# Constant matmuls at the start, early first products, and an earlier third batch in a fused attention and feed-forward kernel

## The chip, the cores and the metric

One core of a Trainium2 chip. The metric is device time in microseconds (us) of one execution. The kernel before took 272.6 us (median of three, 272.22 to 273.03). PE is TensorE, PEld its weight loads, DVE is VectorE, ACT is ScalarE, POOL is GpSimd. "Cold" and "warm" stand for the TensorE clock at half and at full speed (0.5 and 1.0 in the traces' clock record; in the kernel before, weight loads for 512-column matmuls start 0.427 us apart before the record's rise at 27.13 us and 0.214 after it).

## The reference, cut to what matters

Eight batches of attention, eight heads, 576 positions, head size 64. Four heads ("plain") see a window of 32 keys; four ("dilated") see 32 keys at every fourth place. The result, 4608 rows of 512, goes through `((x @ w1) * (x @ w2)) @ w3 @ w_out`.

```python
mask_plain = (rel >= 0) & (rel < window)
mask_dil = (rel >= 0) & (rel < window * dilation) & (rel % dilation == 0)
...
a = x @ w1
b = x @ w2
h = a * b @ w3
return (h @ w_out)
```

## The kernel before

The kernel multiplies w3 by w_out once (`wf`). A token block of 512 rows then needs 64 matmuls of 512 columns for a and b (`ffn1`, f = 0 to 7, four channel groups c each) and 32 for the output (`ffn2`). Each batch's attention is four steps (d0, d1 dilated, p0, p1 plain): scores, exponential, values, normalization on DVE, then six transposes on PE and a copy into `XT`. In profile lines `qt` and `kt` are a step's transposed queries and keys, `vd` and `vp` its values, `xo` its normalized output. Channels 2 and 3 of `XT` are the dilated heads, 0 and 1 the plain ones. The first batch runs ahead of everything. Later steps are laid among the feed-forward matmuls by numbered points, two per f or output block.

```python
def first_batch():
    ...                      # scores of d0, d1, p0; values of d0; scores of p1 ...
    d0.to_channels()
    p0.values_of_pair(0)
    p0.values_of_pair(1)
    d1.to_channels()
    p1.values_of_pair(0)
    p1.values_of_pair(1)
    p0.to_channels()         # all four through one PSUM tile, ps_x, and ACT
    p1.to_channels()
...
def ffn1(t, f, point, lo=0, hi=TB):
    for w_sb in (w1_sb, w2_sb):
        point()
        ps = bank()[:, 0 : hi - lo]
        for c in range(DCH):
            nc.tensor.matmul(out=ps, lhsT=w_sb[:, c, f * P : (f + 1) * P], rhs=XT[:, c, ...],
                             start=(c == 0), stop=(c == DCH - 1))
...
(26, d0.values),             # second batch: (point, what)
(28, transpose_qk, 1, 0, 0),
(28, d0.to_channels),
(28, d1.values),
(29, transpose_qk, 1, 0, 1),
(30, p0.scores),
```

The softmax here doesn't subtract the row's maximum and nothing guards it: scores larger than these inputs give would overflow.

## Time and profile before

The time splits at three places: the first weight load of the first feed-forward block, the first load of w3 (the fused weights begin) and the first load of `gt` (the first output block begins).

| stretch before | from | to | length, us |
|---|---|---|---|
| first batch | 0 | 22.49 | 22.49 |
| first feed-forward block | 22.49 | 38.88 | 16.39 |
| fused weights, second batch | 38.88 | 62.17 | 23.3 |
| rest | 62.17 | 270.16 | 207.99 |

The stretch view of the kernel before gives, for each stretch, its length, the busy time of PE, PEld, DVE, ACT and POOL in this order (number of instructions in brackets), the granted clock, the time that DMA packets took as a share of the 16 DMA engines' time (over 1 where packets overlap) and the rate in GB/s:

```profile
0.00:22.49 22.49, 14.47 (x183) 9.32 (x184) 13.48 (x56) 8.40 (x12) 16.99 (x31) 1.00 1.26 161
22.49:38.88 16.39, 15.66 (x68) 6.75 (x66) 4.84 (x7) 5.19 (x9) 4.63 (x7) 1.00 1.17 209
38.88:62.17 23.29, 20.79 (x261) 11.94 (x260) 16.21 (x32) 9.28 (x11) 12.71 (x17) 1.00 1.52 194
62.17:270.20 208.03, 201.35 (x1846) 99.58 (x1844) 123.85 (x234) 90.81 (x137) 23.49 (x30) 1.00 0.55 91
```

The first number after each length is PE. It is idle 8.0 us in the first row, 2.5 in the third and 6.7 in the last. The clock column's 1.00 in the first two rows is no reading, as the prediction works out: the record begins at 27.13 us.

### The profile page before, as it was taken

The numbers are of one execution on the slowest core, as the hardware profiler recorded it, in microseconds if no ns is written. First come the engines' busy times: TensorE is split into PE (matmuls) and PEld (weight loads), VectorE is DVE, ScalarE is ACT, GpSimd is POOL, SyncE is SP. The second block draws the span as 40 slices with busy tenths as digits, with TensorE's granted clock in tenths as the row PEclk, the third lists the DMA queues.
The fourth block names the chain that finished last, engine by engine and source line by source line (L and its number), as shares of the span: only waits on it lengthen the run. The fifth ranks groups of instructions, "written<-read, shape, count | busy, mean of one in ns | idle before, by whom it ended". The sixth has DMA issues, their size and how long they took to land.

```text
span 270.2 us, 5648 instructions
## 1 busy us (share of the span) xinstructions
PE 252.3 (93%) x2352; PEld 127.6 (47%) x2352; DVE 158.4 (59%) x329; ACT 113.7 (42%) x167; POOL 57.8 (21%) x84
## 2 busy tenths in 40 slices
PE   0897999979988899999999999999999999999993
PEld 0473445545444455455555455554545544444441
DVE  5552446777598777775776678577836642422420
ACT  1443332533455345544553553454454424323331
POOL 8962236534026113310611060000000000000000
PEclk9999999999999999999999999999999999999999
DMA  6999999999959986969597886310040022014013
GB/s 113 163 193 206 210 206 201 195 181 199 222 87 142 91 177 138 103 126 181 72 76 130 194 72 45 109 50 0 4 130 27 0 62 96 0 39 120 0 38 117
DMA packets 51817, 30.50 MB, mean 113 GB/s; under 512 B 37968, under 2 KB 42064, under 8 KB 51792
## 3 DMA queue, kind: packets, MB, share of 16 engines
q0 software_dynamic: 46160, 20.70, 61.9%
q1 hardware_dynamic: 5632, 9.44, 10.9%
q8 instruction: 18, 0.29, 0.5%
q14 instruction: 7, 0.06, 0.1%
HBM read 41.39 MB, written 9.44 MB: 188 GB/s over the span
## 4 chain that ended last, share of the span: by engine, by line
PE 87%; DVE 7%; ACT 2%; DMA 2%; issue 1%; POOL 0%; POOLq 0%; DVEq 0%
PE f L502 45%; PE f L535 23%; PE ps_a L264 4%; PE ps_x L355 4%; PE f L565 3%; PE ps_a L306 3%; DMA kn<-in_k_dram 2%; PE ps_s L264 2%; DVE xo L314 2%; PE ps_s L280 1%; ACT XT L370 1%; ACT et L294 1%; DVE qt L236 1%; DVE kt L229 1%; DVE et L295 1%; DVE gt L513 1%
## 5 line engine op out<-in xcount | busy, mean ns | idle before, releaser
L502 PE MATMUL f<-XT,w_sb 128*128 128x512 bf16 x576 | 135.9, 383 | 0.7 <-ACT XT L370 0.7
L502 PEld LDWEIGHTS <-w_sb 128*128 128x128 bf16 x576 | 53.4, 98 | 60.1 <-issue 3.5
L513 DVE TENSOR_TENSOR gt<-f,asb 128x512 bf16<-128x512 f32 x72 | 49.4, 687 | 48.3 <-PE f L502 44.0
L512 ACT CAST asb<-f 128x512 bf16<-128x512 f32 x72 | 42.1, 585 | 67.2 <-PE f L502 67.2
L535 PE MATMUL f<-wf_sb,gt 128*128 128x512 bf16 x288 | 68.0, 379 | 0.0
L543 ACT COPY osb<-f 128x512 f32<-128x512 f32 x36 | 21.0, 585 | 50.8 <-PE f L535 50.8
L535 PEld LDWEIGHTS <-gt 128*128 128x128 bf16 x288 | 26.4, 98 | 28.5 <-DVE gt L513 0.4
L294 ACT ACTIVATE et<-ps_a 128x1152 bf16<-128x1152 f32 x28 | 31.7, 1134 | 14.0 <-PE ps_a L264 14.0
L138 POOL DMA_DIRECT2D vd<-in_v_dram x32 | 21.3, 672 | 41.9 <-PE ps_a L306 32.4
L314 DVE TENSOR_TENSOR xo<-ps_a,rcp 96x768 bf16<-96x768 f32 x28 | 26.7, 953 | 1.0
L264 PEld LDWEIGHTS <-kt 32*128 32x128 bf16 x768 | 12.2, 97 | 22.5 <-issue 16.9
L236 DVE STREAM_TRANSPOSE qt<-qn 128x160 uint32<-128x160 uint32 (+1 forms) x64 | 19.6, 423 | 1.3 <-DMA qn<-in_q_dram 1.3
L306 PEld LDWEIGHTS <-et 128*128 128x128 bf16 x384 | 16.9, 102 | 6.9 <-issue 0.5
L295 DVE TENSOR_TENSOR et<-et,mask_pl 128x1152 bf16<-128x1152 bf16 x14 | 10.6, 758 | 12.8 <-ACT et L294 12.8
L295 DVE TENSOR_TENSOR et<-et,mask_di 128x1152 bf16<-128x1152 bf16 x14 | 10.6, 756 | 10.4 <-ACT et L294 10.4
L565 PE MATMUL f<-wo_sb,w3T 128*128 128x512 bf16 x64 | 16.0, 380 | 0.7 <-ACT w3T L557 0.7
L264 PE MATMUL ps_a<-qt,kt 32*128 32x96 bf16 x672 | 12.4, 202 | 4.1 <-DVE xo L314 2.3
L355 PEld LDWEIGHTS <-xo 96*128 96x128 bf16 x192 | 12.3, 102 | 7.7 <-issue 1.1
L313 DVE RECIPROCAL rcp<-ps_a 96x12 f32<-96x12 f32 x28 | 6.3, 224 | 15.4 <-PE ps_a L306 15.4
L355 PE MATMUL ps_x<-ident,xo 96*128 96x96 bf16 x192 | 14.4, 214 | 0.9 <-ACT XT L370 0.7
L114 POOL DMA_DIRECT2D qn<-in_q_dram x10 | 6.6, 662 | 30.5 <-DVE qt L236 26.1
L370 ACT COPY XT<-ps_x 128x576 bf16<-128x576 bf16 x18 | 11.6, 642 | 2.7 <-PE ps_x L355 2.4
(51 smaller groups left out, 129.2 us busy)
## 6 DMA issues: line engine op xcount, KB each, us to landing
qn<-in_q_dram POOLq DMA_DIRECT2D x6, 576.0 KB, 5.5
kn<-in_k_dram POOLq DMA_DIRECT2D x6, 576.0 KB, 8.3
w3n<-in_moe_w_dram POOLq DMA_DIRECT2D x4, 512.0 KB, 17.0
out_dram<-osb SPq DMA_DIRECT2D x8, 256.0 KB, 2.4
vp<-in_v_dram POOLq DMA_DIRECT2D x5, 384.0 KB, 6.3
out_dram<-osb SPq DMA_DIRECT2D x8, 224.0 KB, 2.3
out_dram<-osb SPq DMA_DIRECT2D x8, 192.0 KB, 2.9
out_dram<-osb SPq DMA_DIRECT2D x8, 160.0 KB, 2.6
```

Source lines behind the costliest of these rows:

```text
L236: nc.vector.transpose(out=bass.AP(tensor=o.tensor, offset=o.offset + at, ap=[o.ap[0], [1, n], [9, 16], [step, 2]],), in_=t[:, a0 : a0 + 4 ...
L264: nc.tensor.matmul(out=bank_of(h)[:, c0 : c0 + 96], lhsT=kt[prt, 96 * m : 96 * m + P, c], rhs=rhs, start=(start and c == 0), stop=(c == 1 ...
L294: nc.scalar.activation(out=ev, in_=ps_a[:, :, 0:HALF], func=ACT.Exp, scale=scale)
L295: nc.vector.tensor_tensor(out=ev, in0=ev, in1=mk.unsqueeze(1).to_broadcast([P, 4, HALF]), op=AL.mult)
L306: nc.tensor.matmul(out=out, lhsT=self.et[:, c0 : c0 + P], rhs=rhs, start=True, stop=True)
L314: nc.vector.tensor_tensor(out=xo[0:96].rearrange("p (n k) d -> p n k d", n=n), in0=ov[0:96, :, :, x0 : x0 + D], in1=rcp[0:96].unsqueeze(3) ...
L355: nc.tensor.transpose(out=xo, in_=self.xo[0:96, hp, 2 * m : 2 * m + 2, :], identity=ident[0:96, 0:96],)
L502: nc.tensor.matmul(out=ps, lhsT=w_sb[:, c, f * P : (f + 1) * P], rhs=XT[:, c, t0 + lo : t0 + hi], start=(c == 0), stop=(c == DCH - 1),)
L512: nc.scalar.copy(out=a_sb[:, 0 : hi - lo], in_=ps)
L513: nc.vector.tensor_tensor(out=gts[t][:, f, lo:hi], in0=pss[1], in1=a_sb[:, 0 : hi - lo], op=AL.mult)
L535: nc.tensor.matmul(out=y, lhsT=gts[t][:, f, tb * P : (tb + 1) * P], rhs=wf_sb[:, f, :], start=(f == 0), stop=(f == KFF - 1),)
L565: nc.tensor.matmul(out=wf_ps[ft], lhsT=w3T[ft][:, g, :], rhs=wo_sb[:, g, :], start=(g == 0), stop=(g == KFF - 1),)
```

## The change

It has four parts: 16 constant matmuls that raise the clock early; the first two f of block 0 begun with the dilated channels alone, with p1's transposes in a bank of their own and copied by DVE; w3's first part loaded ahead of wo; and the schedule of the second and third batch moved up. Smaller moves that go with them (the values' PSUM banks, the first fused transposes into `ps_x`, the channel order 2, 3, 0, 1 everywhere) stand in the kernel alone.

```diff
+    def warm_up(n):
+        ps = bank()
+        for _ in range(n):
+            nc.tensor.matmul(out=ps, lhsT=warm[:, 0:P], rhs=warm, start=True, stop=True)
...
     def const_vector():
+        nc.vector.memset(warm, 1.0)
...
-        p0.to_channels()
-        p1.to_channels()
+        pool = four_banks()
+        for f in range(2):
+            for i in range(2):
+                begin(f, i, pool.tile([P, TB], F32, name=f"ps_b{f}{i}"))
+            if f == 0:
+                p0.to_channels()
+        p1.to_channels(bank().bitcast(BF16), nc.vector.tensor_copy)
...
-            (28, transpose_qk, 1, 0, 0),
+            (26, transpose_qk, 1, 0, 0),
+            (27, transpose_qk, 1, 0, 1),
...
-            (29, transpose_qk, 1, 0, 1),
...
+            (36, transpose_qk, 2, 1, 0),
             (38, p1.to_channels),
+            (38, transpose_qk, 2, 1, 1),
...
-            if i == lo:
-                later(transpose_qk, b, 1, 0)
-                later(transpose_qk, b, 1, 1)
...
+    def begin(f, i, ps):
+        begun[f, i] = ps
+        ffn1_half(0, f, (w1_sb, w2_sb)[i], (2, 3), begun[f, i])
...
+    warm_up(16)
...
+    load_w3(0)
     load_wo(0)
     load_wo(1)
-    load_w3(0)
...
-    marks = [(40, n0)]
+    marks = [(39, n0)]
```

## The prediction

> **What bounds the kernel now.** I read the page first, then the timeline of each engine over the first 100 us, then when each load landed. The page says that TensorE (PE) is the bound: busy 93% of a 270.2 us span, and the chain that ended last is 87% PE. From 100 us on, PE is busy in all of every stretch, and the change leaves that work alone. What can be won lies in the first 100 us.
>
> ```profile
> PE   0897999979988899999999999999999999999993
> PEld 0473445545444455455555455554545544444441
> DVE  5552446777598777775776678577836642422420
> ACT  1443332533455345544553553454454424323331
> ...
> DMA  6999999999959986969597886310040022014013
> ```
>
> These are tenths busy in 40 slices of 6.8 us. PE's gaps are all in the first 14 slices. The DMA engines are full from 5 us to about 65 us, at some 200 GB/s. "Busy" hides a second loss, which the weight loads of the first feed-forward block give away:
>
> ```profile
> 23.88 0.15 PEld L502 LDWEIGHTS <-w_sb 128*128 128x128 bf16 x1 [0.27 <-issue]
> 24.31 0.15 PEld L502 LDWEIGHTS <-w_sb 128*128 128x128 bf16 x1 [0.27 <-issue]
> ...
> 26.44 0.15 PEld L502 LDWEIGHTS <-w_sb 128*128 128x128 bf16 x1 [0.28 <-issue]
> 26.87 0.15 PEld L502 LDWEIGHTS <-w_sb 128*128 128x128 bf16 x1 [0.27 <-issue]
> 27.22 11.54 PEld L502 LDWEIGHTS <-w_sb 128*128 128x128 bf16 x54 [0.20 <-issue]
> ```
>
> The columns are start, length, engine, line, operation. Each load goes with one 512-column matmul. Up to 27.1 us they start 0.427 us apart; the next 54 take 11.54 us, 0.214 each. So PE runs at half speed until 27 us, although the page's clock row shows full speed throughout (the trace's clock record begins only at 27.13 us). The small attention matmuls between 7.8 and 18.2 us, back to back, did not raise it. The cost in the first block is its 15.75 us for 64 matmuls against 64 x 0.216 = 13.8, so 1.9 us; in the attention before it about half of each matmul.
>
> The third loss is the end of the first batch, a ping-pong of PE and ScalarE on one PSUM tile:
>
> ```profile
> 20.77 0.64 PE L355 MATMUL ps_x<-ident,xo 96*128 96x96 bf16 x6
> 21.44 0.64 ACT L370 COPY XT<-ps_x 128x576 bf16<-128x576 bf16 x1 [0.73 <-PE ps_x L355]
> 22.13 0.64 PE L355 MATMUL ps_x<-ident,xo 96*128 96x96 bf16 x6 [0.73 <-ACT XT L370]
> 22.81 0.64 ACT L370 COPY XT<-ps_x 128x576 bf16<-128x576 bf16 x1 [0.73 <-PE ps_x L355]
> 23.50 2.72 PE L502 MATMUL f<-XT,w_sb 128*128 128x512 bf16 x6 [0.73 <-ACT XT L370]
> ```
>
> Later PE stands still for kt of the second batch, and for VectorE's normalization of the third:
>
> ```profile
> 58.67 0.44 PE L264 MATMUL ps_a<-qt,kt 32*128 32x96 bf16 x24 [1.84 <-DVE kt L229]
> ...
> 79.36 0.44 PE L264 MATMUL ps_a<-qt,kt 32*128 32x96 bf16 x24 [0.76 <-DVE xo L314]
> ...
> 84.73 0.45 PE L264 MATMUL ps_a<-qt,kt 32*128 32x96 bf16 x24 [0.75 <-DVE xo L314]
> ...
> 90.11 0.45 PE L264 MATMUL ps_a<-qt,kt 32*128 32x96 bf16 x24 [0.75 <-DVE xo L314]
> ```
>
> [...] dense matmuls from 23.50, change at 27.13, 3.6 us later. [...] measured 427 and 214 to 216. [...] No trace here shows what load of small matmuls keeps a raised clock up; that is my main doubt.
>
> **The change, part by part.**
>
> *Warm-up.* VectorE fills a 128x512 tile first (near the 0.27 us of the trace's 32x256-word fill), so PE can start 16 matmuls at about 1.15 us instead of waiting for the first mask at 4.41. By the spacing above, all cold is 16 x 0.427 = 6.8 us; with the rise after some 5 us, 12 x 0.427 + 4 x 0.216 = 6.0. They end at 7.2 (at worst 8.0), and kt is ready only at 7.75. So they are hidden, and the scores then run warm.
>
> *First batch, if the clock stays up.* Scores need 0.6 to 0.65 us per pair instead of 1.18, then ScalarE's exponentials (0.65 each) set the pace. The plain heads' scores wait for kt, whose transpose runs 10.71 to 11.97 behind the load of k, so they gain only 12.54 - 12.0 = 0.5 us. The values of the plain heads need v, which landed at 15.88 us in the trace; before, PE came to them at 18.47. So they go at 15.9: 2.5 us won, the rest forbidden by DMA. The second dilated copy to XT then ends near 17.3 (before: 20.7).
>
> *Begun products.* After the split, 8 of the 64 matmuls (channels 2 and 3, the dilated heads) of f = 0 and 1 go into the four banks freed by the scores, among the plain heads' transposes; the last copy has its own bank and VectorE. The first weight slices landed at 17.22 (w1) and 18.56 (w2), so the second half-product waits to 18.56. Then: its 2 matmuls to 19.0, p0's six transposes to 19.3 (copy beside it to 19.95), 4 matmuls to 20.15, p1's transposes to 20.45, copy to 21.1. The other 56 matmuls take 56 x 0.216 = 12.1 us: end at 33.2 to 33.3, against 39.25. Later weights (w1 23.78, w2 26.33 for f = 4) come in time: f = 4 begins at 21.1 + 24 x 0.216 = 26.3. **Won: 5.9 us.**
>
> *Fused weights and second batch.* w3's first part now goes ahead of wo; the three parts trade landings 28.87, 31.40 and 33.91, in time for 33.3. The next w3 parts landed at 36.37, 41.69 and 46.20; PE would need them at about 36.6, 41.6 and 46.8, so there is no slack but no real wait. k of the second batch landed at 49.02; its transpose stands earlier in VectorE's order and ends near 50.5 instead of 58.6, where PE needs it at 50.9. So the 1.84 us wait goes, but VectorE sits on these loads with casts queued behind, which costs PE some 0.5 us. **Won: 1.3 us**, the stretch shrinking from 23.15 to about 21.9.
>
> *Third batch sooner.* Scores of the third batch move into the end of the first output block, and the matmuls between values and next scores go from 4 to 8 twice; 4 x 0.216 = 0.86 us covers two of the 0.75 us waits. The first wait (0.76) stays or grows: two transposes (2.2 us) lie in VectorE's queue ahead of the normalization in both kernels. **Won: about 1.1 us.**
>
> *Sum*: 5.9 + 1.3 + 1.1 = 8.3 us. The rest of the run has the same instructions. 272.6 - 8.3 = 264.3.
>
> **The rivals.**
> 1. *The clock falls back before the dense matmuls.* For: 10 us of small matmuls at full issue left it low, and in the new kernel PE idles from 10.4 to 12 and works half the time after. If it falls at once, the first batch runs as before up to d1's copy, with that at 20.2 to 20.7; the begun products cost 0.427 each, and the 56 end at about 37.8: 1.45 us won, and with nearly 2 us for the kt wait and 1.1 for the third batch about 4.7 in all, 267.9. If it falls only near 15 us, behind the wait for v, the loss is about 1.4 us: 265.7. [...]
> 2. *Loads take over.* The DMA engines are full to 65 us, so PE 6 us earlier meets landings that do not move. I counted v, w2 and k; if w3 or the third batch's q (54.3) and k (57.1) also bite, 1 to 2 us go: 266.
> 3. *VectorE becomes the bound* between 47 and 70 us: busy 8.1 of 10 us in 50 to 60 before, and the same work goes into less time. A wait of 1.5 us instead of 0.76 before the third batch's plain scores: 265.
>
> Nothing added lies on the path of the last 170 us, so slower is very unlikely.
>
> **Range and chances.** I give the warm case half, a late fall 30%, an early fall 20%: 0.5 x 264.3 + 0.3 x 265.7 + 0.2 x 267.9 = 265.4; the warm case being the most likely, I choose 264.9. The 2% mark is 267.1, near the early-fall case alone, so faster gets 0.84. The low end is the warm case with every wait gone (1.9 us more), the high end the early fall.
>
> **What would show it.** Warm-up matmuls from about 1.2 us whose spacing falls to 0.216; score matmuls at about half of 0.59 us per dozen; the plain values released by v at about 15.9; a PE wait on w_sb before the second begun product; the first fused-weight transpose near 33.3; no kt wait near 51; one wait on xo instead of three after 60. Spacing of 0.427 in the begun products means rival 1; waits on w3n or qn mean rival 2; a longer span after 100 us would break the whole account.

The spacings in ns are those of 512-column matmuls in the profile of the kernel before: 0.427 us up to 27.1 us, then 54 loads in 11.54 us, or 0.214 each; from 224.60 us on, 64 matmuls take 13.81 us, or 0.216 each, which the sums use. That the clock would rise after some 5 us of constant matmuls was my estimate; the trace shows one rise, 3.6 us after the dense matmuls began.

## The result, and the profile after

The changed kernel took 265.88 us (median of four: 265.95, 265.93, 265.83, 263.61) against 272.81 (272.22 to 273.16). The ratio is 0.9728, 95% interval 0.9673 to 0.9783. Ratios here are the mean time of one kernel's runs over that of the other's of the same rounds, so not quite the ratio of the medians. Executions over 1.5% slower than the fastest of the same kernel are left out of the means. Three runs lie within 0.12 us with a mean granted clock of 0.981. The fourth is 2.3 us faster with 1.000.

The stretch view of the changed kernel (a 0.981 run), same columns:

```profile
0.00:19.37 19.37, 16.40 (x188) 9.55 (x189) 12.18 (x52) 7.51 (x11) 15.23 (x28) 0.82 1.26 154
19.37:35.88 16.51, 15.62 (x79) 7.32 (x79) 7.03 (x15) 5.45 (x10) 5.18 (x8) 0.91 1.21 209
35.88:57.88 22.00, 20.57 (x257) 12.01 (x260) 16.11 (x32) 9.28 (x11) 10.71 (x14) 1.00 1.42 196
57.88:264.20 206.32, 198.76 (x1816) 99.61 (x1844) 123.77 (x234) 90.37 (x137) 26.64 (x34) 1.00 0.59 96
```

The first two stretches together end 3.00 us sooner (38.88 to 35.88), the third is 1.29 shorter (23.30 to 22.01) and the rest 1.69 (207.99 to 206.30). The sum is 5.98, all of 270.16 - 264.19 = 5.97 but for rounding. The clock column now shows a loss in the first two rows. The page's slices of 6.6 us show where:

```profile
PE   7798999999899999999999999999999999999993
...
PEclk9957999999999999999999999999999999999999
```

The clock is up, then down in the third and fourth slice, then up. The trace's clock record gives the moments: full speed from 5.43 us, half from 12.26, full again from 22.50. The timeline of PE weight loads (start, length) and then of PE matmuls shows the same in the spacing:

```profile
4.85 0.15 PEld L179 LDWEIGHTS <-warm 128*128 128x128 bf16 x1 [0.28 <-issue]
5.28 1.26 PEld L179 LDWEIGHTS <-warm 128*128 128x128 bf16 x6 [0.28 <-issue]
```

```profile
11.77 0.43 PE L275 MATMUL ps_s<-qt,kt 32*128 32x96 bf16 x12 [0.78 <-DVE kt L240]
...
12.64 0.66 PE L275 MATMUL ps_s<-qt,kt 32*128 32x96 bf16 x12
...
17.39 0.86 PE L317 MATMUL f<-vp,et 128*128 128x65 bf16 x12
...
20.48 1.06 PE L509 MATMUL ps_b<-XT,w_sb 128*128 128x512 bf16 x2 [0.22 <-issue]
...
23.99 1.90 PE L509 MATMUL ps_b<-XT,w_sb 128*128 128x512 bf16 x8 [0.55 <-DVE XT L380]
```

The last six warm-up loads take 1.26 us, 0.21 each, where those before stood 0.43 apart. A dozen score matmuls took 0.43 us at 11.77 and 0.66 at 12.64. The plain values at 17.39 waited for nothing: v had landed at 16.77, but PE, cold again, was still busy with the scores and the first transposes. Five of the eight begun matmuls ran cold too, and a sixth in part. The waits further on, from the same timeline:

```profile
54.38 0.45 PE L275 MATMUL ps_a<-qt,kt 32*128 32x96 bf16 x24 [0.56 <-DVE xo L325]
...
72.47 0.44 PE L275 MATMUL ps_a<-qt,kt 32*128 32x96 bf16 x24 [0.94 <-DVE xo L325]
...
77.90 0.44 PE L275 MATMUL ps_a<-qt,kt 32*128 32x96 bf16 x24
...
83.32 0.44 PE L275 MATMUL ps_a<-qt,kt 32*128 32x96 bf16 x24
```

The 1.84 us wait for kt has become 0.56 for the normalization (xo), which DVE takes up after kt. Of three waits on xo in the third batch, one is left, somewhat longer.

### The profile page after: what moved, and what is told of

It is laid out like the page before. It is cut to its first block, busy times and chain, and to the rows that moved or that the text cites. A ratio compares the mean times of both kernels' runs of the same rounds, so it can differ in the third digit from the quotient of the medians.

```text
span 264.2 us, 5646 instructions
## 1 busy us (share of the span) xinstructions
PE 251.4 (95%) x2332; PEld 128.5 (49%) x2368; DVE 159.1 (60%) x331; ACT 112.6 (43%) x166; POOL 57.8 (22%) x84
## 4 chain that ended last, share of the span: by engine, by line
PE 86%; DVE 5%; DMA 2%; ACT 2%; issue 2%; POOL 1%; POOLq 0%
PE f L509 45%; PE f L560 23%; PE ps_a L275 4%; PE ps_a L317 3%; PE f L591 3%; PE ps_x L366 3%; DMA kn<-in_k_dram 2%; PE ps_b L509 2%; DVE xo L325 1%; DVE kt L240 1%; DVE qt L247 1%; ACT et L305 1%; DVE et L306 1%; PE ps_s L275 1%; PE f L317 1%
## 5 line engine op out<-in xcount | busy, mean ns | idle before, releaser
L509 PE MATMUL f<-XT,w_sb 128*128 128x512 bf16 x538 | 128.9, 379 | 1.3 <-issue 0.2
L540 DVE TENSOR_TENSOR gt<-f,asb 128x512 bf16<-128x512 f32 x70 | 48.1, 687 | 39.5 <-PE f L509 35.2
L539 ACT CAST asb<-f 128x512 bf16<-128x512 f32 x70 | 41.0, 586 | 62.5 <-PE f L509 59.8
L560 PE MATMUL f<-wf_sb,gt 128*128 128x512 bf16 x279 | 66.3, 379 | 1.0 <-issue 0.8
L140 POOL DMA_DIRECT2D vd<-in_v_dram x32 | 21.3, 670 | 43.0 <-PE ps_a L317 33.3
L275 PEld LDWEIGHTS <-kt 32*128 32x128 bf16 x768 | 11.4, 94 | 17.6 <-issue 14.1
L591 PE MATMUL f<-wo_sb,w3T 128*128 128x512 bf16 x60 | 15.4, 380 | 0.9 <-ACT w3T L583 0.7
L366 PE MATMUL ps_x<-ident,xo 96*128 96x96 bf16 x186 | 13.8, 213 | 0.1
L380 ACT COPY XT<-ps_x 128x576 bf16<-128x576 bf16 x17 | 10.9, 643 | 3.5 <-PE ps_x L366 3.4
```

Of the source, the lines that this page charges most:

```text
L275: nc.tensor.matmul(out=bank_of(h)[:, c0 : c0 + 96], lhsT=kt[prt, 96 * m : 96 * m + P, c], rhs=rhs, start=(start and c == 0), stop=(c == 1 ...
L366: nc.tensor.transpose(out=xo, in_=self.xo[0:96, hp, 2 * m : 2 * m + 2, :], identity=ident[0:96, 0:96],)
L539: nc.scalar.copy(out=a_sb, in_=ps)
L540: nc.vector.tensor_tensor(out=gts[t][:, f], in0=pss[1], in1=a_sb, op=AL.mult)
L560: nc.tensor.matmul(out=y, lhsT=gts[t][:, f, tb * P : (tb + 1) * P], rhs=wf_sb[:, f, :], start=(f == 0), stop=(f == KFF - 1),)
L591: nc.tensor.matmul(out=wf_ps[ft], lhsT=w3T[ft][:, g, :], rhs=wo_sb[:, g, :], start=(g == 0), stop=(g == KFF - 1),)
```

## The experiments

They ran in three calls (e0 to e3, e4 to e7, e8 to e11). Each kernel ran six times, beside eleven runs of the kernel before in each call, whose means were 272.29, 272.04 and 271.82 us.

**Theory A.** The clock falls in the first batch in most executions (in the profile after at 12.26 us, 6.83 us after its rise), because PE is too thinly filled there. This costs the changed kernel some 2 us, and the schedule of batches two and three gives a fixed 3 us. **Rivals:** the loads set the pace, or the warm-up alone carries the gain.

**e0: the changed kernel again.**

> The changed kernel once more, beside the three runs of this call. Theory A (the TensorE clock falls in the first batch in most executions[...] and stays up in some): two levels, most near 265.9 us with a mean granted clock of 0.98, some near 263.6 us with 1.00, nothing between. Theory B (the 263.61 us was a chance of the loads): times scattered between 263.5 and 266.5 without tie to the clock.

Measured, with mean clock: 263.23 (1.000), 264.57 (0.986), 264.83 (0.986), 265.04 (0.987), 265.85 (0.981), 266.31 us (0.981); ratio 0.9732. There are three levels, not two, and they go with the clock. In the 0.986 profile the clock was up from 6.60 us, down from 13.43, up from 20.25: down for 6.83 us where the 0.981 profile had 10.24. The scatter follows the clock. Of ten runs of the changed kernel, two kept it. (e5 and e6 below leave the first batch as it is; two of six runs of each show 0.998 or more, which makes six of 22.)

**e1: no warm-up.**

```diff
-        nc.vector.memset(warm, 1.0)
...
-    warm_up(16)
```

> The changed kernel without its 16 constant matmuls and their fill. Theory A: where the clock has fallen at 12.3 us anyway, the warm-up saved only the 0.8 us by which the plain scores began sooner, and some of the raise of the clock for the begun products; so about 267 us (266.5 to 268), the clock rising near 24 us, all executions on one level. Theory B (the warm-up carries the gain): over 269 us.

Measured 266.31 us (266.03 to 267.23), ratio 0.9785. It is on one level, as theory A says, but the median is 0.2 us under the expected range and the rise came at 22.52 us, not near 24. The mean, 266.45, is 1.5 us above the changed kernel's 264.97. The clock record begins with that rise and shows no fall in the first batch.

**e2: the kernel before plus the warm-up alone.**

```diff
+        nc.vector.memset(warm, 1.0)
...
+    warm_up(16)          # into a bank of the values
```

> The kernel before plus only the fill and the 16 constant matmuls. Theory A: clock up near 5.5 us and down again near 12.3 us, the first block still begun cold, plain scores 0.8 us sooner: 271.5 to 272.2 us, the same within 2%. If the clock should hold, 3 us more: 268 to 269. Theory B (the warm-up carries the gain): under 268 us.

Measured 269.2 us (268.48 to 271.18), ratio 0.9893. This missed all that was expected but the "should hold" case, which is not quite what happened either: in the profile the clock was up from 4.29 to 17.94 us, past most of the first batch, and down from there to 24.77, over the start of the first block. It fell behind a wait of PE for v (to 16.47), the place that the prediction's late fall had. I had taken the fall at 12.3 us as given; its place shifts from run to run. With the clock up to 17.94, the block ended at 36.38 instead of 38.88. The means give 272.29 - 269.39 = 2.90 us for the warm-up alone, and only 1.5 us on top of the other parts. The two overlap: both bring the first block forward.

**e3: seventeen more constant matmuls inside the first batch.**

```diff
+    def hold(n):
+        for _ in range(n):
+            nc.tensor.matmul(out=ps_x.bitcast(F32), lhsT=warm[:, 0:P], rhs=warm, start=True, stop=True)
...
+        hold(1)   # behind each of the first three score groups
+        hold(4)   # behind the fourth
+        hold(2)   # behind p0's first, d0's values, d1's first values
+        hold(4)   # ahead of d0.to_channels
```

> The changed kernel plus 17 more constant matmuls spread over the first batch (one to four at a time, behind the score and value groups, into the transpose tile while that is unused)[...]. Theory A: the clock stays up from about 5.5 us in every execution; the fillers cost nothing on the path, which waits there for k and v; the first block ends near 34 us instead of 36.1, and the time is 263 to 263.8 us in all runs. Rival (loads set the pace, the clock is beside the point): clock up but still 265.5 us or more. Rival (fillers delay the scores): over 266 us.

Measured 265.03 us (264.85 to 265.81), clocks 0.997 to 1.000, ratio 0.9738. The clock held in all six and the spread shrank, but the time is no better. The fillers are in the way. In DVE's timeline kt of the plain heads was ready at 11.22; the four fillers at 11.20 hold PE to 12.07:

```profile
10.83 0.43 PE L281 MATMUL ps_s<-qt,kt 32*128 32x96 bf16 x12
11.20 1.04 PE L185 MATMUL ps_x<-warm 128*128 128x512 bf16 x4
12.07 0.41 PE L297 MATMUL ps_s<-neg_pl,ident 128*128 128x288 bf16 x2
```

No wait is left anywhere from 8 to 18 us in that timeline: PE itself is the path, fillers included. The block ended at 34.97. So the rival that fillers delay the scores was right in kind.

**e4: no begun products.**

```diff
-                begin(f, i, pool.tile([P, TB], F32, name=f"ps_b{f}{i}"))
+                pool.tile([P, TB], F32, name=f"ps_b{f}{i}")
```

> The changed kernel with no product begun early: all 64 matmuls of the first block after the plain heads' copies (the split over two transpose tiles and the copy on VectorE stay). Theory (the begun products fill the time of the copies and let the clock rise earlier): the block starts near 21 us instead of 19.5, pays some 1.9 us of half clock inside, and ends 0.8 to 1.5 us later than in the changed kernel; about 266.3 us. Rival (they only move work that waits for the weights anyway): no difference beyond 0.3 us from the changed kernel's 265 to 265.9.

Measured 265.39 us, but spread over 263.40 to 267.33 with clocks from 0.978 to 1.000; ratio 0.9756. Inconclusive: the clock's levels cover the difference sought. The profiled run, at 0.979, ended the block at 36.20, 0.32 later than the changed kernel's. e8 asks again with the clock held.

**e5: the third batch as late as before.**

```diff
-            (36, transpose_qk, 2, 1, 0),
-            (38, transpose_qk, 2, 1, 1),
+            if i == lo:
+                later(transpose_qk, b, 1, 0)
+                later(transpose_qk, b, 1, 1)
-    marks = [(39, n0)]
+    marks = [(40, n0)]
```

> The changed kernel with the third batch begun as late as before (its two dilated transposes and its mark put back). Theory: the stretch from the first output matmul to the end, 206.30 us in three profiles of the changed kernel, goes back to about 207.8 (207.99 and 208.02 before), the three waits of some 0.75 us on the normalization come back, and the first two stretches stay: near 266.8 us. Rival (an earlier first block alone removes those waits, as the loads are then no longer late): under 206.8.

Measured 266.51 us (265.65 to 268.04), ratio 0.9799. The rest is 207.99 us in its profile, to the hundredth what it was before, and PE's timeline has the three waits again:

```profile
74.02 0.44 PE L275 MATMUL ps_a<-qt,kt 32*128 32x96 bf16 x24 [0.75 <-DVE xo L325]
...
79.39 0.45 PE L275 MATMUL ps_a<-qt,kt 32*128 32x96 bf16 x24 [0.74 <-DVE xo L325]
...
84.77 0.44 PE L275 MATMUL ps_a<-qt,kt 32*128 32x96 bf16 x24 [0.75 <-DVE xo L325]
```

The earlier third batch is worth 1.69 us in that stretch, and no other part of the change gives it.

**e6: the second batch's plain transposes at their old points.**

```diff
-            (26, transpose_qk, 1, 0, 0),
-            (27, transpose_qk, 1, 0, 1),
+            (28, transpose_qk, 1, 0, 0),
...
+            (29, transpose_qk, 1, 0, 1),
```

> The changed kernel with the second batch's plain transposes back at their old places (points 28 and 29 instead of 26 and 27). Theory: the stretch of the fused weights, 22.01 us in every changed profile, goes back to 23.2 (23.30 before), with the wait on kt of 1.5 to 1.9 us again; near 266.4 us. Rival (the wait went because the first block ended earlier or because w3 came first): stays at 22.0.

Measured 264.73, 265.41, 267.20 and 268.26 us in four runs, mean 266.40, ratio 0.9793; two more, 268.93 and 269.31 with clocks 0.974 and 0.971. The stretch of the fused weights is 23.51 us, and PE's timeline shows the wait in full:

```profile
53.82 0.44 PE L275 MATMUL ps_a<-qt,kt 32*128 32x96 bf16 x24 [1.84 <-DVE kt L240]
```

So the place in DVE's order makes the 1.3 us (1.50 between these two profiles). The k rows were there in time in both: DVE began that transpose without a wait.

This profile is also the only one of the changed kernel's own first batch with the clock held (up from 4.76 us to the end). The block began at 17.67 and ended at 33.81, and PE met a load:

```profile
19.39 0.61 PE L509 MATMUL ps_b<-XT,w_sb 128*128 128x512 bf16 x2 [0.96 <-DMA w_sb<-in_moe_w_dram]
```

**e7: a longer start and seven fillers where PE waits.**

```diff
-    warm_up(16)
+    warm_up(19)
...
         d1.scores_of_pair(1)
+        hold(4)
...
         d1.values_of_pair(1)
+        hold(3)
```

> The changed kernel with 19 constant matmuls at the start instead of 16 and only 7 more inside, where PE waits anyway: 4 behind the dilated scores, 3 before the first transposes. Theory A: the 17 fillers of the last trial held the clock but cost over 1 us on the path, since the block ended at 34.97 with the clock up, where 33.5 is what the fastest execution of the changed kernel leaves. With few fillers the clock stays up in most executions, the block ends near 33.8 us: 263.2 to 264.2 us, steady. Rival (so few do not hold the clock): [...] two levels as in the changed kernel, median 265.

Measured 263.94 us (263.25 to 264.22), clocks 0.996 to 1.000, ratio 0.9701 (0.9660 to 0.9741). Time and clock are as theory A says. The gain over the changed kernel (264.94 in e0, of another call) is about 1 us, with overlapping intervals; that the spread is smaller is plain. Its first two stretches:

```profile
0.00:17.76 17.76, 14.93 (x195) 8.24 (x198) 11.69 (x51) 7.26 (x11) 15.11 (x28) 1.00 1.25 150
17.76:33.15 15.39, 14.37 (x81) 6.78 (x79) 7.34 (x15) 5.68 (x10) 4.58 (x8) 1.00 1.24 207
```

The block ends at 33.15, sooner than the 33.8 expected here, where the prediction's warm case had 33.2 to 33.3; the later stretches are 22.02 and 206.3 as in the changed kernel.

**e8: e7 without begun products** (the edit of e4 on e7).

> The held clock of e7 without any product begun early. Theory (with the clock up, eight begun matmuls of 0.216 us fill only what the copies leave, and they in turn push the plain transposes back): the first block starts near 19.6 us and ends within 0.5 us of e7's 33.15; time 263.8 to 264.5 us, not told apart from e7's 263.94. Rival (the begun products are a main part of the gain): 265 us or more.

Measured 264.07 us; the four runs with clocks of 0.998 or more took 263.31 to 264.27, two with 0.991 and 0.992 took 265.37 and 266.26; ratio 0.9729. With the clock up, the begun products are worth nothing that these runs resolve: the block started at 19.57 and ended at 33.51, 0.36 after e7's. That the clock sagged in two of six runs, and in none of e7's, may mean that they help to keep it; six runs don't settle it.

**e9: e7 with wo ahead of w3.**

```diff
-    load_w3(0)
     load_wo(0)
     load_wo(1)
+    load_w3(0)
```

> The held clock of e7 with wo loaded ahead of w3's first part, as before the change. Theory: in e7 the block ends at 33.15 and w3's first part landed at 28.53; behind wo it would land where wo's second half did, near 33.6, so the first fused transpose waits 0.3 to 1.4 us: 264.2 to 265.2 us, with a wait on w3n in the profile and the span of that stretch up from 22.01. Rival (the order is of no account): 263.94 within 0.2.

Measured 263.87 us (263.39 to 265.57), ratio 0.9714: as a median no different from e7. The profiled run was the longest of the six, at 265.57, and shows where it waited:

```profile
16.54 0.49 PE L323 MATMUL f<-vp,et 128*128 128x65 bf16 x11 [0.28 <-DMA vp<-in_v_dram]
...
19.21 0.61 PE L517 MATMUL ps_b<-XT,w_sb 128*128 128x512 bf16 x2 [0.52 <-DMA w_sb<-in_moe_w_dram]
...
35.66 0.62 PE L585 MATMUL ps_x<-ident,w3n 128*128 128x128 bf16 x8 [1.35 <-DMA w3n<-in_moe_w_dram]
```

Here v landed at 16.50, w2 at 19.17 and w3 at 35.62 us, and PE, warm, met all three. In the changed kernel's profile v (16.77) and w2 (19.45) were no sooner, but with the new order w3 landed at 29.69; so the order guards against the third wait. The other five runs, 263.39 to 263.89, show no cost. By its number the rival was right: 263.94 within 0.2. The wait that the theory expected is there in the one profile, but ahead of the fused stretch, which at 21.82 us did not grow.

**e10: e7 with one more begun half-product.**

```diff
         p1.to_channels(bank().bitcast(BF16), nc.vector.tensor_copy)
+        begin(2, 0, bank())
```

> e7 plus one more begun half-product (f = 2, w1), in a free bank behind the last transposes, where PE waits 0.55 us for VectorE's copy. Theory: two matmuls of 0.216 us go into that wait, as w1's second slice landed at 19.52: 0.4 us off e7, 263.3 to 263.7 us. Rival (the slice lands late in many executions, or the copy is delayed): no gain.

Measured 263.3 us (262.91 to 264.24), clocks 0.998 to 1.000, ratio 0.9695 (0.9654 to 0.9736). The block ends at 32.78, 0.37 sooner than e7's. It has the lowest median here, but its lead on e7, of another call, and on the changed kernel is within the intervals.

**e11: nineteen constant matmuls at the start, none inside.**

> The changed kernel with 19 constant matmuls at the start and none inside: parts e7. Theory A [...]: two levels remain, clocks from 0.98 to 1.00, median 264.5 to 265.5. Rival (the longer start alone holds the clock): all at 263.3 to 264.2 with clocks over 0.995.

Measured 264.41 us: 263.06, 263.33 and 263.85 with clocks of 0.996 or more, 264.97, 265.02 and 265.81 with 0.986, 0.994 and 0.981; ratio 0.9725. The longer start alone does not hold the clock. With fillers inside and begun products it held in all 24 runs of e3, e7, e9 and e10, and e3 did it with the short start; without the begun products (e8) in four of six. This profile, with the clock up to 259.64 us, again meets v, which landed at 15.85, and the second weight slice:

```profile
15.89 0.49 PE L317 MATMUL f<-vp,et 128*128 128x65 bf16 x11 [0.47 <-DMA vp<-in_v_dram]
...
18.60 0.61 PE L509 MATMUL ps_b<-XT,w_sb 128*128 128x512 bf16 x2 [0.63 <-DMA w_sb<-in_moe_w_dram]
```

## Why the prediction was right or wrong

The time, 265.88, lies between the warm case with every wait gone (262.4) and the early fall (267.9), and within 1 us of 264.9. "Faster by over 2%" was right for the median. That the middle number fits so well is in part luck: the clock fell more often than allowed for, and the held runs came out some 0.9 us below their 264.3, which offsets it. (The early-fall sum has a slip: 1.45 + 2 + 1.1 is 4.55, not 4.7.) Step by step:

- **Warm-up.** Right in kind. PE began at 1.46 us instead of 1.15, since the fill took 0.48 us and not 0.27. The rise came at 5.43, when PE had run nothing but these matmuls of ones since 1.46; the last warm-up matmul was done near 7.0, and kt was ready just after 7.8. It was hidden.
- **"First batch, if the clock stays up."** This is the step that failed as the usual case. The clock stayed up in two of ten runs of the changed kernel, and I had given it half. Where it held, the account was close: a block end of 33.2 to 33.3 was predicted; 33.81 was measured with the changed kernel's own first batch (e6, where w2 landed 0.8 us later than counted), 33.15 in e7 and 33.02 in e11. The changed kernel's held runs took 263.61 and 263.23 us against 264.3 predicted.
- **"If it falls only near 15 us", rival 1.** This became the usual run. Predicted 265.7; measured 264.57 to 266.31. The chances were misplaced, not the mechanism: I had taken short gaps for harmless, which no trace had shown. The waits between 5.43 and 12.26 us in the profile are 0.61 and 0.78 us, PE was busy for 5.4 of those 6.8 us (2.79 and 2.60 in the halves), and the clock fell all the same, before PE came to v at all.
- **v at 15.9 as the limit of the plain values, and the wait on the second weight slice.** Not seen in the profile after, because PE ran cold and came later than the loads. Seen with the clock up: on v 0.28 us in e9 and 0.47 in e11, at 15.89 as predicted; on w_sb 0.52 in e9, 0.63 in e11 and 0.96 in e6.
- **Begun products.** They were counted within 5.9 us with the warm-up. The first two stretches gave 3.00 in the 0.981 profile. With the clock held, e8 shows nothing in the times that the begun products themselves give (0.36 us at the block's end, one profile of each). Less the 2.98 us of the later stretches (1.29 + 1.69), the first part gained 272.29 - 264.97 - 2.98 = 4.34 us on average; the warm-up alone gives 2.90 (e2), the rest of the change alone 272.29 - 266.45 - 2.98 = 2.86 (e1). They overlap by 1.42.
- **Fused weights, 1.3 us.** Measured 1.29. The two sides of it were also right: the 1.84 us on kt went, and 0.56 on the normalization behind kt came, predicted as some 0.5. e6 shows that the place of the transposes does it.
- **Third batch, 1.1 us.** Measured 1.69, so mis-sized by 0.6. Two of three waits on xo went and the first stayed, longer by 0.18, as predicted. e5 shows the part alone. These waits make 0.75 + 0.75 - 0.18 = 1.32; the rest I can't assign to a single wait.
- **Rival 2, loads.** Not in the usual run, but once the clock is held they are next, as the waits in e6, e9 and e11 show. **Rival 3, DVE.** Present as the 0.94 and 0.56 us waits, within what had been counted.

What stays open: which property of the load the clock goes by. The spans between two recorded changes of the clock in the profiles before, after, e0 and e2 are multiples of 3.413 us (242.35 up before; 6.83 up, 10.24 down and 242.35 up after; 6.83 and 6.83 in e0; 13.65 and 6.83 in e2), so I cut the traces into windows of that length, 3.41 below. PE's busy time is not it: cut from the rise, e6's trace kept the clock through one with 2.34 us busy, while the changed kernel's fell after one with 2.60. A count made afterwards from all fourteen traces does tell the windows apart. It sums the columns that the matmuls of a window stream, each matmul weighted by the share of PE's 128 rows that it feeds (a score matmul feeds 32; sixteen dense matmuls of 512 columns make 8,192). The five full-speed windows before a fall hold 2,360 to 3,050; of those that kept the clock, up to 200 us, none holds under 3,120. At half speed, no rise followed windows of up to 3,090 (the kernel before's small matmuls reach 2,960), and one followed each of 3,210 and more, with two missing records put back. The margin is thin (windows set 0.1 us later close it), and no run was made to test it.

Also open: no run takes away the separate bank and DVE's copy for p1's transposes, so their share of the first part is not shown. Where the record begins with the rise, as in the kernel before, an earlier state can't be read from it: the mean granted clock there is 0.999, although the loads up to 27.1 us stand 0.427 us apart. The kernel before also ran from 269.75 to 273.16 us; whether the same cause lies behind that was not tested.

## What to carry to other kernels

After a warm-up, look at whether the clock is still up when the dense work begins, and read it from the spacing of equal matmuls (0.427 or 0.214 us at 512 columns here); in the profile after it fell with no PE wait over 0.78 us. A few constant matmuls laid where the engine waits anyway (seven in e7, with a longer start) held it (0.996 to 1.000 in all six runs) and made the kernel steadier and, as far as runs of different calls tell, some 1 us faster; seventeen, more freely spread (e3), cost what they gained. Where runs fall on several levels, compare stretches that do not depend on the level: here the rest came out between 206.29 and 206.33 us in all eleven profiles with the early third batch and the fused stretch between 21.8 and 22.3 with the early transposes, inside a scatter of 3 us.
